# Loading part of wq on chosen DMA engines: 1152 columns in six loads against 1664 columns in five

## The chip, the cores and the metric

The kernel runs on one core of a Trainium2 chip. The core has five engines that run beside each other: TensorE (PE, with its weight loads shown apart as PEld), VectorE (DVE), ScalarE (ACT), GpSimd (POOL) and SyncE (SP), which here issues nearly all DMA loads. Sixteen DMA engines move the data. The metric is the device time in microseconds (us); lower is better.

## The reference

A decode step for eight sequences of one token each: attention over a cached window, then an MLP, each after a layer norm, each added to its input.

```python
def _A_ref(x, k_cache, v_cache, wq, wo):      # x [8,1,512], 32 query heads, 8 kv heads, Dh 128
    W = min(4096, max(256, Sk // 4))          # Sk = 8192, so the last 2048 positions
    q = (x @ wq)                              # wq [512, 4096]
    k = k_cache[:, :, Sk - W:, :]             # caches [8, 8, 8192, 128], repeated over 4 heads
    v = v_cache[:, :, Sk - W:, :]
    p = _softmax(einsum(q, k) * Dh ** -0.5)
    return einsum(p, v) @ wo                  # wo [4096, 512]

def _B_ref(x, w1, w2, w3, w4):                # the token shift of w1 and w2 is all zero for one token
    x1 = x + hs                               # hs is zero here
    return x1 + _gelu(_layernorm(x1) @ w3) @ w4    # w3 [512,1792], w4 [1792,512]

h = x + _A_ref(_layernorm(x), ...)
return h + _B_ref(_layernorm(h), ...)
```

Everything is bfloat16. Of the caches 64 MB are read, of the weights some 11 MB.

## The kernel before

The work is a stream of loads with the arithmetic behind it. SP issues the loads in an order written out by hand as a string of letters: K and V stand for one 2 MB piece of a cache each (four kv heads of one sequence, 2048 positions), Q for wq and O for the three pieces of wo; w3 and the three pieces of w4 come at the end. The order begins K, Q, K, K, V, K, V. Three buffers for K (knat) and three for V (vnat) are reused in turn, so that a load waits until the transposes (K, line 383) or the second product (V, line 504) of the piece three before are done.

K arrives with positions on the partitions. PE turns it (L383) into PSUM, ACT (L393) and DVE (L395) move it to kT_sb, PE multiplies it with the queries (L408), and after the softmax it multiplies the turned probabilities with V (L504). The result of each sequence is gathered in oW. At the end come wo (L553, L574), the layer norm, w3 (L678), the gelu (L704), w4 (L731), and the store (L788).

The queries need wq first. wq has 512 rows; row 4p+k is put on partition p as one of four stretches of 4096 columns of the tile wbig. The load of wbig leaves out the last QF = 1152 columns of the last stretch, that is, the last 1152 columns of every fourth row of wq (128 such pieces, one for each partition). These 128 pieces are loaded apart, by several small loads, into wqF, a view of the tile of w3, which is still free then.

The table FILL says how. Each entry (k, h, n) is one load of 4k pieces: k is the outer count of the source's access pattern, the pieces go to the partitions 32h to 32h+4k-1, and n is one of NF slots of wqF along the free dimension. With k = 8 a load runs on eight DMA engines, with k = 3 on three. All the other loads have 128 partitions and run on all sixteen. The function fills() walks the table; load_wq issues the loads (the helper at L207 issues every load); q_rows uses the same table three times: it copies the matching columns of the normalised x into xlnP (L282), turns them with PE (L287) into the same partitions and slots of xlnF (L292), and multiplies slot by slot with wqF (L313), after the products with wbig (L302), into the same PSUM banks. Partitions of a slot that hold no piece have to be zero in both: POOL clears xlnF (L216) and slots 1 and 2 of wqF (L217) at the start. A load into slot 0 doesn't wait for that, since slot 0 is filled in full; the others do.

The memsets on POOL stand ahead of the iota (L219), from which DVE makes the two identity matrices (L227, L228) and turn_f (L239), which the transposes of K need. q_rows stands on PE behind the transposes of the first four K tiles.

Of the kernel before, what the change touches and what calls it, by code (L numbers as in the profile page):

```python
# [6 lines left out]
dt = mybir.dt  # L7
# [4 lines left out]
B = 8  # L12
D = 512
H = 32
DH = 128
# [9 lines left out]
KC = D // 128  # L25
# [15 lines left out]
QW = H - 2 * NQ * R + 1  # L41
QE = QW + NQ * R + NQ * R + QW
AHEAD = NS
QF = 1152
FILL = ((8, 0, 0), (8, 1, 0), (8, 0, 1), (3, 1, 1), (3, 0, 2), (2, 1, 2))
NF = 3
KF = 64


class Engine:  # L50
# [29 lines left out]
def bass_sequential_preLN__sliding_block_cached__mixer_s_mlp__decode_kernel(  # L80
# [23 lines left out]
    with es:  # L104
        sb = lambda shape, dtype, name: es.enter_context(nc.sbuf_tensor(name, shape, dtype))
# [34 lines left out]
        rstd = sb([B, 1], dt.float32, "rstd")  # L140

        xlnF = sb([KF, NF, 32], dt.bfloat16, "xlnF")
        xlnP = sb([B, 4 * sum(k for k, _, _ in FILL)], dt.bfloat16, "xlnP")
        wqF = w3_sb[0:KF, 2:4, :].rearrange("p a n -> p (a n)")[:, 0:NF * QF].rearrange("p (s n) -> p s n", s=NF)
        xlnT = sb([128, KC, 32], dt.bfloat16, "xlnT")
        qrow = sb([128, 2, 512], dt.bfloat16, "qrow")
# [52 lines left out]
        sem_wf = S("sem_wf")  # L199
# [3 lines left out]
        PE, AC, DV, PO, SP = (Engine(S(n)) for n in ("s_pe", "s_act", "s_dve", "s_pool", "s_sp"))  # L203

        def dma(eng, dst, src, sem, *waits):
            def f(e):
                e.dma_start(dst, src).then_inc(sem, 16)  # L207
            eng.op(f, *waits, inc=False)
# [5 lines left out]
        PO.op(lambda e: e.memset(eps2[:], EPS * EPS))  # L214
        e_scr = PO.op(lambda e: e.memset(scratch[:], 1.0))
        e_fz = PO.op(lambda e: e.memset(xlnF[:], 0.0))  # L216
        e_wz = PO.op(lambda e: e.memset(wqF[:, 1:NF, :], 0.0))  # L217
        e_xz = PO.op(lambda e: e.memset(xlnT[:], 0.0))
        e_iota = PO.op(lambda e: e.iota(iota_f[:], [[1, 128]], base=0, channel_multiplier=-1,  # L219
                                        allow_small_or_imprecise_dtypes=True))  # L220
# [8 lines left out]
        e = DV.op(lambda e: e.bn_stats(st6[:, :], x_sb[:, :]), X)  # L229
        e = DV.op(lambda e: e.bn_aggr(mv[:, :], st6[:, :]), e)  # L230
        e = PO.op(lambda e: e.tensor_scalar(rstd[:, :], mv[:, 1:2], EPS, None, ALU.add), e)
        e = PO.op(lambda e: e.tensor_tensor(rstd[:, :], rstd[:, :], half[0:B, 0:1], ALU.pow), e)
# [8 lines left out]
        e = DV.op(lambda e: e.tensor_reduce(hsq[:, :], ident_f[:, :].rearrange("p (u h) -> p h u", u=4), AX.X, ALU.add))  # L241
# [7 lines left out]
        e = DV.op(lambda e: e.tensor_reduce(rows16[:, :].rearrange("p (t r) -> p t r", t=KQ),  # L249
                                            rows_f[:, :].rearrange("p (t s r) -> p t r s", t=KQ, s=NS), AX.X, ALU.add))  # L250
        a = rows16[:, :]
# [11 lines left out]
        e = PE.op(pe_xT, e_xln, e_idb)  # L263
# [5 lines left out]
        qT_ps = (o_rows, sm)  # L269
        fT_ps = pT_ps[:, 128:128 + NF * B]  # L270

        def fills():
            at = 0
            for k, h, n in FILL:
                yield k, slice(32 * h, 32 * h + 4 * k), n, at, slice(at, at + 4 * k)
                at += 4 * k

        def q_rows():
            for k, rows, n, at, where in fills():
                a = xln_b[:, :]  # L280
                cols = bass.AP(tensor=a.tensor, offset=a.offset + KC * at + KC - 1, ap=[a.ap[0], [KC, k], [KC * k, 4]])
                e_xP = DV.op(lambda e, cols=cols, where=where: e.tensor_copy(  # L282
                    xlnP[:, where].rearrange("b (e a) -> b e a", a=4), cols))

            def pe_fT(e):
                for k, rows, n, at, where in fills():
                    ins = e.matmul(fT_ps[rows, n * B:(n + 1) * B], xlnP[:, where], ident_b[0:B, 0:B],  # L287
                                   is_transpose=True, tile_position=(0, rows.start))
                return ins
            e = PE.op(pe_fT, e_xP)  # L290
            for k, rows, n, at, where in fills():
                e_fT = DV.op(lambda e, rows=rows, n=n: e.tensor_copy(xlnF[rows, n, 0:B], fT_ps[rows, n * B:(n + 1) * B]),  # L292
                             e, e_fz)
            out = []
            for j in range(2):
                def pe_q(e, j=j):
                    for kc in range(KC):
                        for u in range(4):
                            n = (4 * j + u) * R * DH
                            size = R * DH if kc < KC - 1 else max(0, min(R * DH, H * DH - QF - n))  # L300
                            if size:
                                ins = e.matmul(S_ps[j][32 * u:32 * (u + 1), 0:size], xlnT[:, kc, :], wq_v[:, kc, n:n + size],  # L302
                                               start=(kc == 0), stop=(kc == KC - 1 and size == R * DH),
                                               tile_position=(0, 32 * u), skip_group_check=True)
                    return ins

                def pe_qF(e):
                    for n in range(NF):
                        for u in range(4):
                            w = (u - 4) * R * DH + QF  # L310
                            lo = max(0, -w)
                            if lo < R * DH:
                                ins = e.matmul(S_ps[1][32 * u:32 * (u + 1), lo:R * DH], xlnF[:, n, :],  # L313
                                               wqF[:, n, w + lo:w + R * DH], start=False, stop=(n == NF - 1),
                                               tile_position=(0, 32 * u), skip_group_check=True)
                    return ins
                e_q = PE.op(pe_q, e_xT, (sem_wq, 16))
                if j == 1:
                    e_q = PE.op(pe_qF, e_fT, (sem_wf, 16 * len(FILL)))
                got = S_ps[j][:, :].rearrange("p (r d) -> p r d", r=R)  # L320
                for c in range(2):
                    if j == 0:
                        e = AC.op(lambda e, c=c, got=got: e.activation(qrow2[:, 0, :, c, :], got, ACT.Copy, scale=inv_sqrt_dh),
                                  e_q)
                    else:
                        e = DV.op(lambda e, c=c, got=got: e.tensor_scalar(qrow2[:, 1, :, c, :], got, inv_sqrt_dh, None,
                                                                          ALU.mult), e_q)
                out.append(e)
            return out, e_q
# [149 lines left out]
        a = ident_f[:, :].bitcast(dt.bfloat16)  # L479
# [126 lines left out]
        for p in range(AHEAD):  # L606
            pe_T(p)
            evict(p)
        e_qrow, e_q = q_rows()
        e_qT, e_qturn = q_turn()  # L610
        fill(0)
# [33 lines left out]
        def bc(a):  # L645
            return bass.AP(tensor=a.tensor, offset=a.offset, ap=[a.ap[0], [0, KC], [1, B]])


        e = DV.op(lambda e: e.tensor_reduce(hsum[:, :], vr(hT_ps[:, 0:NH]), AX.X, ALU.add), e_wo[-1])
# [41 lines left out]
        e = AC.op(lambda e: e.activation(s2[:, :], vsum[:, :], ACT.Sqrt, bias=eps2[:, :], scale=1.0), e_vs)  # L691
        e_r2 = DV.op(lambda e: e.reciprocal(r2[:, :], s2[:, :]), e)

        def bcf(t):
            a = t[:, :]
            return bass.AP(tensor=a.tensor, offset=a.offset, ap=[a.ap[0], [0, FH], [1, B]])
# [3 lines left out]
        for n in range(2):  # L700
            cs = slice(n * FH * B, (n + 1) * FH * B)
            e = DV.op(lambda e, n=n, cs=cs: e.tensor_tensor(v3(g_x[:, cs]), v3(y_ps[n][:, 0:FH * B]), bcf(r2),
                                                            ALU.mult), e_y[n], e_r2)
# [3 lines left out]
        e = PO.op(lambda e: e.tensor_scalar(r1[:, :], vsum[:, :], EPS * (1.0 + EPS), None, ALU.add), e_vs)  # L707
        e = PO.op(lambda e: e.tensor_tensor(r1[:, :], r1[:, :], half[:, :], ALU.pow), e)
        e = DV.op(lambda e: e.tensor_tensor(v3(xb[:, :]), v3(hc[:, :]), bc(r1[:, :]), ALU.mult), e)
# [49 lines left out]
        def load_wq():  # L759
            size = KC * H * DH - QF  # L760
            dma(SP, wbig[:, 0:size], A_wq.rearrange("(p k) n -> p (k n)", k=KC)[:, 0:size], sem_wq)
            for k, rows, n, at, where in fills():
                dma(SP, wqF[rows, n, :],
                    bass.AP(tensor=A_wq.tensor, offset=A_wq.offset + (KC * at + KC - 1) * H * DH + H * DH - QF,
                            ap=[[KC * H * DH, k], [KC * k * H * DH, 4], [1, QF]]), sem_wf, e_wz if n else None)

        def load_w3():
            dma(SP, w3_sb[:, :, :], B_w3.rearrange("(k p) f -> p k f", p=128), sem_w3, e_qturn)
# [8 lines left out]
        for kind in "KQKK" + 9 * "VK" + "VKKVKVKVVVOVOO":  # L777
            if kind == "Q":
                load_wq()
                continue  # L780
            {"K": load_k, "V": load_v, "O": load_wo}[kind](turn[kind])
            turn[kind] += 1
# [42 lines left out]
```

## Time and profile before

| | us |
|---|---|
| median of 3 runs | 193.34 (193.27 to 194.32) |
| the profiled execution: time | 193.18 |
| its span, first to last instruction | 191.9 |
| landing of the big load of wq (issued 1.42) | 17.53 |
| first product with the queries (L408) | 24.99 |
| landing of w3 | 185.03 |
| landing of the last piece of w4 | 189.32 |
| issue of the store | 190.50 |

| engine | busy us | share of the span |
|---|---|---|
| PE | 151.5 | 79% |
| DVE | 102.5 | 53% |
| ACT | 95.7 | 50% |
| POOL | 30.3 | 16% |

How to read it: the page of a profile divides the span into 40 slices and prints one digit a slice, tenths of busy time; 9 is 90% or more. The row DMA is the mean busy share of the 16 DMA engines. In the chain of work that ended last a row gives start, duration and what ran; a DMA's row runs from its issue to its landing. A row of the timeline gives start, duration, engine, line and operation, the tile written and the tiles read, and in brackets the idle time before it with what ended it. The trace also has a record of each DMA packet, with its queue, start, duration and size, and the times at which each load's semaphore counts up, once for every DMA engine that took part; neither names the engine.

### The profile page before, as it was taken

What the parts mean: (1) busy time and instruction counts of PE and PEld (TensorE: products, weight loads), DVE (VectorE), ACT (ScalarE), POOL (GpSimd) and SP (SyncE); (2) the same over time, 40 slices, a digit from 0 to 9 for tenths busy, and PEclk for the clock granted to TensorE, in tenths of its full rate; (3) what the DMA queues carried; (4) which work ended last, traced back from release to release, by engine and by line L of the source; (5) the groups of instructions that cost most, each with busy time, mean ns of one, the idle gap of its engine ahead of it and who ended that gap; (6) DMA issues with size and microseconds to landing.
All of it is one profiled execution on the core that took longest, in us unless ns stands there. A gap on an engine that the chain in (4) does not pass through costs nothing.

```text
span 191.9 us, 3209 instructions
## 1 busy us (share of the span) xinstructions
PE 151.5 (79%) x1325; PEld 94.9 (49%) x1325; DVE 102.5 (53%) x245; ACT 95.7 (50%) x124; POOL 30.3 (16%) x65
## 2 busy tenths in 40 slices
PE   0293879988878998699978896989898994777874
PEld 0281247664546555465655463746554661323453
DVE  2754314773386438543775275646853885535323
ACT  3081127776272927284559263754782767420331
POOL 8300020100230023002300230024002200140030
PEclk9999769999996999889999997999999999999985
DMA  6999999999999999999999999999999999999991
GB/s 220 422 406 432 437 420 427 434 437 424 434 429 427 430 430 427 429 430 430 437 430 420 437 430 429 420 437 424 437 434 425 434 434 432 408 430 428 411 409 75
DMA packets 6478, 79.38 MB, mean 414 GB/s; under 512 B 688, under 2 KB 704, under 8 KB 1856
## 3 DMA queue, kind: packets, MB, share of 16 engines
q1 hardware_dynamic: 6448, 79.18, 97.2%
q8 instruction: 10, 0.16, 0.3%
q14 instruction: 4, 0.03, 0.0%
q10 hardware_dynamic: 16, 0.01, 0.0%
HBM read 79.18 MB, written 0.01 MB: 413 GB/s over the span
## 4 chain that ended last, share of the span: by engine, by line
DMA 65%; PE 22%; DVE 6%; ACT 4%; SPq 1%; issue 1%; POOL 0%
DMA knat<-in_A_k_cache_dram 31%; DMA w_sb<-in_B_w_dram 16%; DMA vnat<-in_A_v_cache_dram 10%; PE kT_ps L383 9%; DMA wbig<-in_A_wq_dram 8%; PE S_ps L504 3%; ACT pT_sb L472 2%; PE S_ps L408 2%; PE o_rows L504 2%; DVE kT_sb L395 2%; ACT kT_sb L393 1%; PE S_ps L302 1%; PE sm L529 1%; PE kT_ps L678 1%; SPq L207 1%
## 5 line engine op out<-in xcount | busy, mean ns | idle before, releaser
L393 ACT ACTIVATE kT_sb<-kT_ps 128x1024 bf16<-128x1024 bf16 x64 | 65.6, 1025 | 65.3 <-PE kT_ps L383 65.2
L383 PE MATMUL kT_ps<-turn_f,knat 128*128 128x128 f32 x512 | 76.5, 293 | 12.2 <-DMA knat<-in_A_k_cache_dram 9.6
L383 PEld LDWEIGHTS kT_ps<-turn_f,knat 128*128 128x128 f32 x512 | 60.4, 149 | 31.9 <-issue 13.4
L395 DVE COPY kT_sb<-kT_ps 128x1024 bf16<-128x1024 bf16 x64 | 43.9, 686 | 34.7 <-PE kT_ps L383 34.6
L516 POOL TENSOR_TENSOR omask<-omask 128x256 f32<-128x256 f32 x14 | 10.2, 726 | 113.3 <-DVE omask L514 113.3
L408 PE MATMUL S_ps<-kT_sb,qblk 128*32 128x512 bf16 x256 | 26.5, 408 | 1.7 <-POOL qblk L350 1.1
L504 PE MATMUL o_rows<-vnat,pT_sb 128*64 128x512 bf16 x128 | 15.4, 381 | 5.4 <-ACT pT_sb L472 5.4
L472 ACT ACTIVATE pT_sb<-o_rows,own_f 128x512 bf16<-128x512 f32 x28 | 17.7, 694 | 1.8 <-PE o_rows L467 1.6
L504 PE MATMUL S_ps<-vnat,pT_sb 128*64 128x512 bf16 x112 | 13.4, 382 | 0.7 <-DMA vnat<-in_A_v_cache_dram 0.7
L504 PEld LDWEIGHTS o_rows<-vnat,pT_sb 128*64 128x64 bf16 x128 | 8.0, 109 | 11.5 <-issue 7.7
L408 PEld LDWEIGHTS S_ps<-kT_sb,qblk 128*32 128x32 bf16 x256 | 6.6, 93 | 13.4 <-issue 8.3
L514 DVE TENSOR_TENSOR omask<-o_rows,own_s 128x512 f32<-128x512 f32 x7 | 4.8, 686 | 12.5 <-PE o_rows L504 12.5
L514 DVE TENSOR_TENSOR omask<-S_ps,own_s 128x512 f32<-128x512 f32 x7 | 4.8, 692 | 11.7 <-PE S_ps L504 11.7
L350 POOL COPY qblk<-qT 64x64 bf16<-64x64 bf16 x16 | 5.0, 312 | 27.0 <-DVE qT L342 16.4
L504 PEld LDWEIGHTS S_ps<-vnat,pT_sb 128*64 128x64 bf16 x112 | 5.8, 110 | 6.8 <-issue 1.6
L529 PE MATMUL sm<-oacc,sel_o 128*128 128x256 f32 x16 | 7.2, 537 | 0.6 <-DVE oX L536 0.6
L440 ACT ACTIVATE E_sb<-S_ps,negM 128x512 f32<-128x512 f32 x8 | 5.5, 689 | 2.4 <-DVE negM L436 2.4
L259 PE MATMUL sm<-ident_b,xln_b 8*128 8x8 bf16 x4 | 0.3, 176 | 8.0 <-DVE xln_b L234 8.0
L517 POOL TENSOR_TENSOR oacc<-omask 128x128 f32<-128x128 f32 x14 | 6.4, 455 | 1.1
L559 ACT ACTIVATE orow<-kT_ps 128x512 bf16<-128x512 f32 x1 | 0.6, 597 | 11.2 <-PE kT_ps L553 11.2
L431 DVE TENSOR_REDUCE mblk<-S_ps 128x1 f32<-128x512 f32 x8 | 5.5, 682 | 0.8 <-PE S_ps L408 0.8
L453 DVE STREAM_TRANSPOSE PT_sb<-P_sb 128x512 bf16<-128x512 bf16 x8 | 5.6, 702 | 0.0
(120 smaller groups left out, 102.6 us busy)
## 6 DMA issues: line engine op xcount, KB each, us to landing
knat<-in_A_k_cache_dram SPq DMA_DIRECT2D x16, 2048.0 KB, 19.3
vnat<-in_A_v_cache_dram SPq DMA_DIRECT2D x15, 2048.0 KB, 20.3
wbig<-in_A_wq_dram SPq DMA_DIRECT2D x1, 3808.0 KB, 16.1
wbig<-in_A_wo_dram SPq DMA_DIRECT2D x2, 1024.0 KB, 22.9
knat<-in_A_v_cache_dram SPq DMA_DIRECT2D x1, 2048.0 KB, 20.4
wbig<-in_A_wo_dram SPq DMA_DIRECT2D x1, 2048.0 KB, 24.7
w_sb<-in_B_w_dram SPq DMA_DIRECT2D x1, 1792.0 KB, 30.7
w_sb<-in_B_w_dram SPq DMA_DIRECT2D x1, 1024.0 KB, 32.6
```

Of the source, the lines that this page charges most:

```text
L383: ins = e.matmul(kT_ps[i % 2][:, n * 256:(n + 1) * 256].bitcast(dt.float32), knat[:, j % NK, c * DH:(c + 2) * DH].bitcast(dt.float32), tur ...
L393: e_lo[i] = AC.op(lambda e: e.activation(kT_sb[:, i % NKT, 0:W // 2], kT_ps[i % 2][:, 0:W // 2], ACT.Copy), e_Tlo[i], e_QK.get(i - NKT))
L395: e_hi[i] = DV.op(lambda e: e.tensor_copy(kT_sb[:, i % NKT, W // 2:W], kT_ps[i % 2][:, W // 2:W]), e_Thi[i], e_QK.get(i - NKT))
L408: ins = e.matmul(S_ps[b % 2][32 * t:32 * (t + 1), :], qblk[:, b % 2, KQ * q + t, half, at:at + H], kT[:, :, t, :, half], start=(q == 0 and ...
L431: e = DV.op(lambda e: e.tensor_reduce(mblk[:, 0:1], S_ps[b % 2][:, :], AX.X, ALU.max), e_QK[G * b + G - 1], e_mz)
L453: e_PT[b] = DV.op(lambda e: e.transpose(PT_sb[:, :], P_sb[:, :]), e_P[b], e_wide.get(b - 1))
L472: e_pT[b, t] = AC.op(lambda e: e.activation(pT_sb[:, b % 2, :, H * t:H * (t + 1)], bank[:, :].rearrange("p (n y) -> p n y", n=NN), ACT.Cop ...
L504: ins = e.matmul(bank[64 * u:64 * (u + 1), :], pT_sb[:, b % 2, n, :].rearrange("p (x q) -> p q x", q=NQ)[:, q, :], v_tile(m)[:, n * 512:(n ...
L514: free[at] = DV.op(lambda e: e.tensor_tensor(omask[:, :, :], bank.rearrange("p (s d) -> p s d", s=NS), own, ALU.mult), e_PV[m], e_acc.get( ...
L516: e = PO.op(lambda e: e.tensor_tensor(omask[:, 0:2, :], omask[:, 0:2, :], omask[:, 2:4, :], ALU.add), free[at], pool[-1])
L517: pool[-1] = e_acc[m] = PO.op(lambda e: e.tensor_tensor(acc, omask[:, 0, :], omask[:, 1, :], ALU.add), e, e_O.get(b - 2))
L529: e_O[b] = PE.op(lambda e: e.matmul(O_ps, sel_o[:, :], oacc[:, b % 2, :, :].rearrange("p q d -> p (q d)"), start=True, stop=True), e_acc[N ...
```

## The change

QF grows from 1152 to 1664 columns, so the big load has 512 columns fewer. FILL's entries get a fourth number m, the pieces for each step of the outer count, which was always 4. The table has five loads instead of six: two of twelve times four pieces (partitions 0 to 47 and 64 to 111 of slot 0), two of three times four (partitions 0 to 11 and 32 to 43 of slot 1), and one of eight single pieces (partitions 64 to 71 of slot 1). There are two slots instead of three, and they reach over 128 partitions instead of 64. As slot 0 is no longer full, all of wqF is cleared, and every load apart waits for that.

```diff
-QF = 1152
-FILL = ((8, 0, 0), (8, 1, 0), (8, 0, 1), (3, 1, 1), (3, 0, 2), (2, 1, 2))
-NF = 3
-KF = 64
+QF = 1664
+FILL = ((12, 4, 0, 0), (12, 4, 2, 0), (3, 4, 0, 1), (3, 4, 1, 1), (8, 1, 2, 1))
+NF = 2
+KF = 128
...
-        e_wz = PO.op(lambda e: e.memset(wqF[:, 1:NF, :], 0.0))
+        e_wz = PO.op(lambda e: e.memset(wqF[:, :, :], 0.0))
...
-            for k, h, n in FILL:
-                yield k, slice(32 * h, 32 * h + 4 * k), n, at, slice(at, at + 4 * k)
-                at += 4 * k
+            for k, m, h, n in FILL:
+                yield k, m, slice(32 * h, 32 * h + m * k), n, at, slice(at, at + m * k)
+                at += m * k
...
-                            ap=[[KC * H * DH, k], [KC * k * H * DH, 4], [1, QF]]), sem_wf, e_wz if n else None)
+                            ap=[[KC * H * DH, k], [KC * k * H * DH, m], [1, QF]]), sem_wf, e_wz)
```

The uses of fills() in q_rows take m in place of the 4 in the same way.

## The prediction

> **What bounds the kernel now.** I read the page's forty slices first, then its DMA parts, the chain that ended last and the timeline at both ends, and last the single DMA packet records and landing counts of the trace.
>
> ```profile
> DMA  6999999999999999999999999999999999999991
> ...
> DMA packets 6478, 79.38 MB, mean 414 GB/s; under 512 B 688, under 2 KB 704, under 8 KB 1856
> ...
> q8 instruction: 10, 0.16, 0.3%
> q14 instruction: 4, 0.03, 0.0%
> ```
>
> The DMA engines have no free slice between the first and the last: bytes set the pace. The two instruction queues look negligible here and are not, as the packet records show below. The chain's end, and the timeline there:
>
> ```profile
> 154.37 30.67 DMA w_sb<-in_B_w_dram
> 185.03 0.05 issue
> 185.08 1.99 PE kT_ps L678 x56
> ...
> 188.99 0.80 PE S_ps L731 x20
> ```
>
> ```profile
> 189.36 0.14 PEld L731 LDWEIGHTS S_ps<-w_sb,qrow 128*32 128x32 bf16 x8 [0.21 <-DMA w_sb<-in_B_w_dram]
> 189.82 0.56 ACT L741 ACTIVATE orow<-S_ps 8x128 bf16<-8x128 f32 x2 [2.23 <-PE S_ps L731]
> 189.82 0.60 DVE L743 CAST orow<-S_ps 8x128 bf16<-8x128 f32 x2 [1.74 <-PE S_ps L731]
> 190.50 0.32 SPq L788 DMA_DIRECT2D out_dram<-orow  x1
> ```
>
> The W3 load releases L678 at 185.03, and the last piece of W4 (landed 189.32) releases the last eight matmuls at 189.36. Both are landings in one ring order, so the end follows the engine that lands last.
>
> The packet records tell which one that is. A load is cut over its engines; each engine runs its packets back to back, each starting 3 or 4 ns before the one ahead ends (16,384 B take 611 ns on every engine, in nearly all of 4,234 packets). So the records fall into 16 chains, and the number of 2,304-byte rows sorts them. End of each chain's last packet in us (the landing follows 0.29 later):
>
> ```
> 24 rows, two engines (0, 1)      188.29  188.88
> 20 rows, one engine (2)          188.30
> 12 rows, five engines (3 to 7)   187.13  187.30  188.49  188.80  188.84
> no row, eight engines (8 to 15)  186.09  186.47  187.51  187.54  187.63  187.68  187.69  189.03
> ```
>
> The numbers 0 to 15 are my labels by how many loads a chain takes part in. Within a class the ends differ by instruction fetches: a 16 KB packet of q8 sets its chain back 1.41 us (186.09 against 187.51), an 8 KB one of q14 0.55 to 0.85. Ten q8 packets go round eight chains: two of class 3 to 7, then six of class 8 to 15. The first, at 26.66, hits the fifth of those six, and the ninth, at 180.90, hits it again. That chain, with no row at all, is the one at 189.03, which ends the kernel; the tenth fetch comes at 187.62, too late to matter.
>
> **The change part by part.** The time of the profiled execution is 193.18, of which 191.9 is span; the median of the runs shown is 193.34, 0.16 above, and I carry differences over to that.
>
> The big load of wq loses 512 columns a row: 30,464 B at 1,128 ns against 16,384 at 611 is 0.0367 ns a byte, so 1,024 B less save 38 ns, and eight rows an engine save 0.30 us on all sixteen.
>
> The rows apart have 3,328 B. No packet of that size exists; on the line through 4,096 B (159 ns) and 3,584 B (140 ns) it takes 131 ns, less the 3.5 of overlap 127; the old row takes 93, so 89.5. Engines 0 to 2 get 4+4+4+4+1 = 17 rows, 3 to 7 get 9, 8 to 11 get 8, 12 to 15 none. New against old:
>
> - 0, 1: 17×127 = 2.16 for 24×89.5 = 2.15, with the 0.30: -0.28
> - 2: 2.16 for 1.79: +0.08
> - 3 to 7: 1.14 for 1.07: -0.23
> - 8 to 11: 1.02 for nothing: +0.72
> - 12 to 15: -0.30
>
> That holds if a row costs the same whoever else is writing. In the old loads apart engine e writes partitions 4e to 4e+3 or the same 32 above, and no other engine does either. The new twelve-engine loads are different. In the first, engines 8 to 11 write partitions 32 to 47, beside engines 0 to 3 at 0 to 15. In the second, all twelve write 64 to 111, the half that engines 8 to 15 fill in every full load, four of which are then on K rows already. In the last, eight engines write eight neighbouring partitions. Before shows no such row. Bounds: from below nothing (eight engines write x into eight neighbouring partitions at 44 ns a packet, unstretched); from above the output store, where eight engines read eight such partitions and the 1,024-byte packets take 45 to 101 ns, a factor of 2.3. I take a factor of 2, two writers that halve one place: x is one short packet an engine, which may hide a queue, while here each engine puts four rows of 3,328 B on end. It costs:
>
> - 0, 1, 2: eight rows doubled, 1.02, and their last single row, one of four at one place, some 0.25: +0.99, +0.99, +1.35
> - 3: as much, +1.04; 4 to 7: four rows doubled against the K rows of 12 to 15, 0.51, and 0.25: +0.53
> - 8 to 11: eight rows, 1.02: +1.74, on two of them up to 0.5 more
> - 12 to 15: 0.51 lost while shared: +0.21
>
> The new ends: 188.88+0.99 = 189.87; 188.30+1.35 = 189.65; 188.84+0.53 to 1.04 = 189.4 to 189.9; 187.69+1.74 to 2.24 = 189.4 to 189.9; 189.03+0.21 = 189.24. Several land together near 189.9 and the latest of so many lies a little above: 190.08 against 189.03, +1.05. The tail behind the last landing is unchanged work and moves with it.
>
> The Trainium skill, "SBUF — State Buffer", section "Door 1: The DMA port swizzle", states that partitions 32 apart share one of 16 DMA ports of about 27 GB/s and that 64 partitions get no more bandwidth than 32. By that rule the sharing above is real and the sum is about the +1.05; the trace of before neither shows nor denies it, for its rows apart kept to their own places.
>
> What goes away on compute: one matmul of 512 columns at L302, one of 128 at L313, one transpose, two small DVE copies. All lie in the stretch that waits for wq; none bears on the end, for the loads never wait for them. The other parts that the change touches stand at the start:
>
> ```profile
> 0.94 2.02 POOL L217 MEMSET w_sb<- 64x2304 bf16 x1
> ...
> 2.03 4.55 SPq L207 DMA_DIRECT2D w_sb<-in_A_wq_dram  x6
> ...
> 3.15 0.24 POOL L219 IOTA iota_f<- 128x128 f32 x1
> ...
> 6.63 1.23 SPq L207 DMA_DIRECT2D knat<-in_A_k_cache_dram  x2
> ...
> 8.59 5.60 PE L383 MATMUL kT_ps<-turn_f,knat 128*128 128x128 f32 x32 [0.26 <-DVE turn_f L239]
> ...
> 14.21 0.54 SPq L207 DMA_DIRECT2D knat<-in_A_k_cache_dram  x1
> ...
> 17.57 2.85 PE L302 MATMUL S_ps<-wbig,xlnT 128*32 128x512 bf16 x30 [1.86 <-DMA wbig<-in_A_wq_dram]
> ```
>
> The memset grows from 2,304 to 3,328 elements a partition: 2.02×1.44 = 2.92, ending 3.86. Now every load apart waits for it, and behind that wait on SP stand K1, K2, V0. Five issues at 0.72 end near 7.5 instead of 6.58, so K1 is issued 0.9 late; engines run on K0 and the big load until about 16.7, a cover of 9 us. On POOL the iota, the identities made from it on DVE, turn_f and the first transposes (L383) all slip 0.9; K3's issue, behind them, goes from 14.21 to 15.1, while V0 occupies the rings until 33.97. L287 moves to 16.4, ahead of wq's landing at 17.2. Each cost is zero; without the covers the largest would be 0.9. If the rows apart land 1 us later than L302 needs, QK starts up to 0.7 late, and K4's issue (32.24) with it; V1 occupies the rings until 43.68, so again nothing.
>
> **The rivals.** *Rows do not share* (not slower): the writes go in at the engines' own rate, as x's packets do. Then the last chains are 188.73 (the one with two fetches, if it is among 12 to 15) and 188.60: -0.30, 193.04, inside the bound. It decides if the new rows show 131 ns throughout.
>
> *The fetches fall elsewhere.* I put the twice-hit chain among 12 to 15 because the round goes upward: after two of 3 to 7 it is the fifth of six, hence at least 12. If the changed program's round begins elsewhere, or goes downward, the double hit falls on one of 8 to 11: 189.03+0.72, 194.06, without sharing; 189.03+1.74 to 2.24, 195.1 to 195.6, with it. The spread of the runs, 194.32 beside 193.27, is about what a double hit on class 3 to 7 would make (187.1+2.82 = 189.9), so the round may well move from one execution to another.
>
> *No double hit that counts, and no sharing*: the last would be engine 0 or 1 without fetch, 188.29-0.28 = 188.01, -1.02 on 189.03: 192.3.
>
> That the load isn't spread as said speaks from no row: the old loads fall into exactly the classes their outer counts name.
>
> **How the numbers follow.** A measurement of this kernel can tell about 0.5%, 0.97 us. Sharing with the round as it is: 0.45, time 193.34+1.05 = 194.4, own range 193.8 (half as dear) to 194.7 (factor 2.3); 0.27 of it above the bound, 0.18 below. No sharing: 0.21, same. Round moved without sharing: 0.07, same; with sharing 0.20, slower. No hit that counts: 0.07, faster. Sums: slower 0.47, same 0.46, faster 0.07. The range 193.0 to 195.3 leaves out the last case and half of the dear one.
>
> **What would show it.** In the changed profile: 3,328-byte packets of engines 0 to 3 and 8 to 11 at 131 or near 260 ns; K1's landings spread by about 3.5 us instead of 2.25 (21.98 to 24.23); which class ends last; the last landing near 190.4. A last landing at or below 189.3 proves the sharing wrong. A PE wait for knat that is much longer than now before 60 us would show that a cover failed.

## The result and the profile after

The changed kernel takes 193.79 us (median of 22 runs, 193.59 to 194.05), the kernel before 193.32 (22 runs): 0.47 us more, a ratio of 1.0021 with a 95% interval of 1.0015 to 1.0027. The profiled executions differ by 0.61 (193.79 against 193.18). The forecast was +1.05. A ratio, here and below, is worked out from the fast runs of both kernels and is not the ratio of the two medians; the only slow runs are two of second_at_64, 197.62 and 201.02 us.

The page of the changed kernel, the rows of the DMA engines and of the instruction queues:

```profile
DMA  6999999999999999999999999999999999999992
...
DMA packets 6484, 79.38 MB, mean 412 GB/s; under 512 B 694, under 2 KB 710, under 8 KB 1862
...
q8 instruction: 10, 0.16, 0.3%
q14 instruction: 4, 0.03, 0.0%
```

Still no free slice, the same bytes, 14 instruction fetches as before. Its chain that ended last, and the end of its timeline:

```profile
154.66 31.02 DMA w_sb<-in_B_w_dram
185.72 1.99 PE kT_ps L678 x56
188.37 1.05 PE S_ps L731 x32
189.63 0.79 PE S_ps L731 x24
```

```profile
189.99 0.14 PEld L731 LDWEIGHTS S_ps<-w_sb,qrow 128*32 128x32 bf16 x8 [0.20 <-DMA w_sb<-in_B_w_dram]
190.45 0.56 ACT L741 ACTIVATE orow<-S_ps 8x128 bf16<-8x128 f32 x2 [2.22 <-PE S_ps L731]
190.45 0.59 DVE L743 CAST orow<-S_ps 8x128 bf16<-8x128 f32 x2 [1.74 <-PE S_ps L731]
191.14 0.31 SPq L788 DMA_DIRECT2D out_dram<-orow  x1
```

The chain is the same as before, each step 0.63 to 0.69 later: the last eight matmuls start at 189.99 instead of 189.36, the last landing is at 189.95 instead of 189.32. So the whole difference is in when the DMA engines land their last bytes. Where it arises is seen in the windows around the rows apart and K1 (the last three numbers of a row are the granted clock of TensorE, the mean busy share of the DMA engines, and GB/s counted by packets that start in the window). Before, then after:

```profile
16.50:22.00 5.50, 4.43 (x41) 1.57 (x42) 0.43 (x3) 1.08 (x2) 0.00 (x0) 0.69 0.99 417
22.00:26.00 4.00, 2.06 (x17) 0.88 (x16) 1.64 (x4) 0.00 (x0) 1.25 (x4) 0.90 1.02 438
26.00:189.00 163.00, 138.20 (x1215) 86.91 (x1218) 90.45 (x208) 88.53 (x114) 22.87 (x43) 0.95 1.00 425
```

```profile
16.50:22.00 5.50, 3.27 (x46) 1.50 (x46) 2.36 (x13) 1.09 (x2) 0.00 (x0) 1.00 1.05 387
22.00:26.00 4.00, 2.54 (x19) 1.81 (x20) 0.76 (x3) 0.24 (x1) 1.24 (x4) 0.86 0.98 418
26.00:189.00 163.00, 136.45 (x1187) 84.72 (x1188) 90.53 (x208) 88.04 (x114) 22.94 (x43) 0.95 1.00 427
```

From 26 us on the two are alike. Between 16.5 and 22 the engines are as busy as before (1.05 against 0.99), yet move 387 GB/s instead of 417: packets take longer. The single packets say how. Of the 128 rows of 3,328 B, 71 take 131 ns, the rest up to 336. And K1, eight packets of 16,384 B on each engine, takes 4.87 us on every chain of before (8 times 607, and the semaphore packet). A chain is, as in the prediction, the packets of one engine in a row. In the changed kernel K1 takes:

```
chains by first packet of K1     K1, us         end of last packet, us (before: by class)
four at 16.60 to 16.72 (12-15)   5.64           186.76 188.06 188.19 189.67   (0 rows: 186.09 to 189.03)
nine at 17.68 to 18.00 (3-11)    5.26 to 5.66   187.50 to 189.28              (0 and 12 rows)
three at 19.31 to 19.38 (0-2)    4.89 to 4.90   188.60 189.14 189.22          (20, 24 rows: 188.29 188.30 188.88)
```

All packets of rows and K1 together have 12.2 us of excess over 131 and 611 ns, a mean of 0.76 for each of the 16 chains; chain by chain it is some 0.6 to 1.0. The last chain is again one of 12 to 15 that is fetched on twice (at 27.81 and 181.41), 189.67. On it the big load ends 0.25 earlier than on the last chain of before, K1 takes 0.77 longer, and the first fetch sets it back by 1.52 instead of 1.41: together the 0.63 by which the end moved. Why that fetch costs more is not shown; it costs 1.52 to 1.58 in every kernel here that writes the rows elsewhere than before does, and 1.41 in before, start_only and before_pause.

### The profile page after: what moved, and what is told of

Its sections match the earlier page's. It is cut to its first block, busy times and chain, and to the rows that moved or that the text cites. A ratio compares the mean times of both kernels' runs of the same rounds, so it can differ in the third digit from the quotient of the medians.

```text
span 192.5 us, 3200 instructions
## 1 busy us (share of the span) xinstructions
PE 150.4 (78%) x1322; PEld 95.2 (49%) x1322; DVE 102.3 (53%) x243; ACT 95.5 (50%) x124; POOL 31.2 (16%) x65
## 4 chain that ended last, share of the span: by engine, by line
DMA 65%; PE 19%; DVE 5%; ACT 5%; POOL 2%; SPq 2%; issue 1%; POOLq 0%
DMA knat<-in_A_k_cache_dram 32%; DMA w_sb<-in_B_w_dram 16%; DMA vnat<-in_A_v_cache_dram 10%; PE kT_ps L383 8%; DMA w_sb<-in_A_wq_dram 7%; PE S_ps L504 3%; ACT pT_sb L472 2%; ACT kT_sb L393 2%; PE o_rows L504 2%; PE S_ps L408 2%; DVE kT_sb L395 2%; SPq L207 2%; POOL w_sb L217 1%; PE kT_ps L678 1%; PE S_ps L731 1%
## 5 line engine op out<-in xcount | busy, mean ns | idle before, releaser
L383 PEld LDWEIGHTS kT_ps<-turn_f,knat 128*128 128x128 f32 x512 | 61.1, 150 | 33.1 <-DMA knat<-in_A_k_cache_dram 15.3
L504 PE MATMUL o_rows<-vnat,pT_sb 128*64 128x512 bf16 x128 | 15.9, 390 | 5.9 <-ACT pT_sb L472 5.9
L529 PE MATMUL sm<-oacc,sel_o 128*128 128x256 f32 x16 | 6.6, 502 | 0.6 <-DVE oX L536 0.6
```

The costliest lines, as they stand in the source:

```text
L383: ins = e.matmul(kT_ps[i % 2][:, n * 256:(n + 1) * 256].bitcast(dt.float32), knat[:, j % NK, c * DH:(c + 2) * DH].bitcast(dt.float32), tur ...
L504: ins = e.matmul(bank[64 * u:64 * (u + 1), :], pT_sb[:, b % 2, n, :].rearrange("p (x q) -> p q x", q=NQ)[:, q, :], v_tile(m)[:, n * 512:(n ...
L529: e_O[b] = PE.op(lambda e: e.matmul(O_ps, sel_o[:, :], oacc[:, b % 2, :, :].rearrange("p q d -> p (q d)"), start=True, stop=True), e_acc[N ...
```

## The experiments

All times are beside runs of before on the same chip, with the ratio to them. Experiments on the loads write FILL as (k, m, first partition, slot); the code around it is that of the changed kernel, with its longer memset and its waits, and q_rows turns a load that starts at partition 32 and reaches over 64 in two pieces. The diffs show the lines that matter, cut at "...", with the old FILL in the same form.

**start_only: the start without the loads.**

```diff
+QF = 1152
+FILL = ((8, 4, 0, 0), (8, 4, 32, 0), (8, 4, 0, 1), (3, 4, 32, 1), (3, 4, 0, 2), (2, 4, 32, 2))
+NF = 3
```

> The loads of before (2,304-byte rows, the same destinations), but wqF cleared over all 128 partitions and every load apart waiting for that, as in the changed kernel. If the later start has its cover, as the prediction has it: 193.3, within 0.1 of before, rows at 93 ns, the last landing at 189.3. If the start itself costs what the changed kernel lost: 193.8.

Measured 193.56 against 193.41, ratio 1.0003 (0.9982 to 1.0024); its profiled execution took 193.31, with 113 of 128 rows at 93 ns, K1 at 4.87 us (4.89 on one chain) and the last landing at 189.36, against 189.32 in before. The start is covered, as forecast.

```profile
16.50:22.00 5.50, 3.57 (x50) 1.68 (x51) 3.10 (x16) 1.21 (x3) 0.00 (x0) 1.00 1.01 420
```

On this chip both kernels had a second level about 0.9 above the first, before in 14 of 35 runs; so the medians say little, and the packets more. The lower level of before, its other 21 runs, has its median at 193.29.

**second_at_64: one of the old loads to the other half.**

```diff
-FILL = ((8, 4, 0, 0), (8, 4, 32, 0), ...
+FILL = ((8, 4, 0, 0), (8, 4, 64, 0), ...
```

> As start_only, and of the first two eight-engine loads the second goes to partitions 64 to 95 instead of 32 to 63; the reads are the same to the byte. Places shared on the write side: engines 0 to 7 then write into the half that the eight engines without rows are filling with K1; four rows of 84 KB in all, about 0.34 us lost on each of the engines 8 to 15 and as much on 0 to 7, some rows well over 93 ns, the last landing 0.3 later, 193.6. Reads by twelve engines at once as the cause of the stretch in the changed kernel: nothing changes, 193.3 and 93 ns.

Measured 194.45, ratio 1.0029 (1.0008 to 1.0051). The reads are those of before to the byte, and still only 61 of 128 rows take 93 ns, against 113 in start_only; others reach 392. So the stretch comes from where the rows are written, not from twelve engines that read. But the loss isn't where it was expected: K1 is long on all 16 chains, 5.4 to 5.5 us. In the profiled execution something more was seen:

```profile
16.50:22.00 5.50, 3.54 (x49) 1.58 (x49) 2.08 (x10) 1.09 (x2) 0.00 (x0) 1.00 1.02 372
22.00:26.00 4.00, 1.82 (x17) 1.09 (x18) 0.77 (x3) 0.00 (x0) 1.25 (x4) 1.00 1.02 393
...
28.00:60.00 32.00, 25.65 (x209) 16.98 (x206) 17.64 (x38) 18.39 (x23) 3.62 (x8) 0.95 1.01 431
```

Long after the last of the rows (19.5), up to 26, the rate stays at 393 and the engines are at 1.02: every packet of every chain takes 675 to 684 ns instead of 611. At 26.51 the first instruction fetch takes one chain out for 1.1 us, and from 26.9 on all the others are at 611 again. So K1's length here is mostly this step (six packets of 70 ns more, some 0.4 of 0.6 us on the chains without rows), and not the meeting of the writes itself. The four runs that lie in the lower level, 193.47 to 193.67, stand some 0.3 above the lower level of before, near the 193.6 that was expected.

**twelve_at_32: the changed loads, other partitions.**

```diff
-FILL = ((12, 4, 0, 0), (12, 4, 64, 0), (3, 4, 0, 1), (3, 4, 32, 1), (8, 1, 64, 1))
+FILL = ((12, 4, 32, 0), (12, 4, 32, 1), (3, 4, 0, 0), (3, 4, 0, 1), (8, 1, 96, 0))
```

> The changed kernel with both twelve-engine loads at partitions 32 to 79 (of slots 0 and 1), the three-engine loads at 0 to 11, the last one at 96 to 103; the reads are those of the changed kernel. If engine e has its own place at 4e to 4e+3 and 32 above (counting 64 to 127 on from there), nobody shares in the two large loads: rows at 131 ns but for the last single ones, engines 12 to 15 no longer held up, and the sum without sharing holds: 0.30 less than before, 193.0. Reads by twelve engines as the cause: rows as stretched as in the changed kernel, 193.8.

```profile
16.50:22.00 5.50, 3.37 (x44) 1.64 (x45) 2.50 (x10) 1.09 (x2) 0.00 (x0) 1.00 1.06 440
```

The profiled execution took 193.01; 440 GB/s in the window; 116 of 128 rows at 131 ns; K1 4.90 us on chains 12 to 15 and on seven of the nine chains 3 to 11 (5.13 and 5.18 on the other two, each with one packet of about 860 ns); last chain 188.87, against 188.73 by the unshared sum. Rows and K1 have 1.5 us of excess in all, against 12.2 in the changed kernel. So the sum without sharing holds once the partitions are right. The times on this chip were in two levels: three runs at 193.0 to 193.1, nine at 193.9 to 194.7, hence a median of 194.02 and a ratio of 1.0011 (0.9988 to 1.0034). What the upper level is, no profile of this kernel caught.

**late_ninth: no second fetch on the last chain.** Of each group of 16 second products of the first seven sequences 12 are left out, so this kernel does not compute the whole result.

```diff
-                for n in range(NN):
+                for n in (range(NN) if b == LAST else (0, 1, NN - 2, NN - 1)):
```

> The changed kernel, leaving out 12 of the 16 second products (L504) of each group in the first seven sequences: 168 matmuls and as many weight loads fewer on PE, so that the ninth 16 KB instruction fetch falls behind the last landing. If the chain that is fetched on twice sets the end: it lands 1.4 earlier, the end passes to the next chain, 0.4 earlier (189.28 against 189.67 in the packet records), 193.4. If the double fetch is no cause: 193.8.

Measured 193.59 (193.27 to 193.87), ratio 0.9996 (0.9979 to 1.0013). That ratio can't be set beside the 1.0021 of the changed kernel, for on this chip 14 of 35 runs of before are in the upper level and none of these 12; beside the lower level of before it is 0.30 more, where the changed kernel had 0.47 and 0.38 more on two other chips. In the packet records no chain has two 16 KB fetches before the end (the eighth comes at 183.77, the ninth at 189.30), and the last chain is now one of 0 to 2, at 189.56. So the twice-fetched chain did set the end of the changed kernel, at 189.67, and the end passed on when its second fetch went. But only 0.11 of the expected 0.4 was gained in this profile, where K1 took 5.70 us instead of 5.64 on the chains without rows; by time alone the difference is too small to show more.

**after_again, and a short pause.** The changed kernel beside before on a third chip, and three kernels with one small load issued on ACT's queue at 18.2 to 19.4 us, two rows of 8 KB on two engines, to see whether it ends the step of 681 ns.

```diff
+                        if c:
+                            dma(AC, w4_sb[0:2, 0:8, :].rearrange("p k n -> p (k n)"),
+                                A_wo.rearrange("(p j) n -> p (j n)", j=8)[0:2, :], sem_b)
```

> The changed kernel as it is, on the chip of this set, beside before. Shared places plus the double fetch: its profile again with about half of the 3,328-byte rows over 131 ns, chains 12 to 15 some 0.6 later than before, 193.7 to 193.9. If the higher level near 194.2 that before showed in 14 of 35 runs of the last set is a property of the chip and not of the kernel, the changed kernel shows it here as well, near 194.6.

> Before, with one small load added on ACT's queue behind L323, at about 19.4: two rows of 8 KB on two engines, into a part of w4's tile that is loaded much later. The profile of second_at_64 had all sixteen chains at 681 ns a packet from about 17.5 until the first instruction fetch at 26.5 took one chain out, then 611 at once. Theory: packets of all engines can fall into a step in which each takes 681, and any short interruption of one engine ends it; this, lasting until the first fetch, is the upper level near 194.2. Then this kernel shows the lower level alone, 193.3 to 193.5, its own cost being 0.3 on two chains that do not end the kernel. Rival, the upper level comes from elsewhere: it stays in about 4 runs of 10.

> second_at_64 with the same small load at 19.4. If a short interruption ends the step of 681 ns: packets at 611 from about 20 on in the profile, and no run above 194.0 (8 of 12 were without it), 193.6. If not: 681 until the first fetch, 194.4.

> twelve_at_32 with the same small load. If its upper runs near 194.1 (9 of 12) were the step of 681 ns: all runs near 193.0 to 193.2, below before by 0.2 to 0.3. If they were something else: two levels as without it.

The diff shows the load alone; the loads of w4 wait for it. On this chip before had one level only (31 runs, 193.17 to 193.61), so the pause had little to end and its theory wasn't tested. after_again: 193.72, ratio 1.0016 (1.0008 to 1.0025), 71 of 128 rows at 131 ns, K1 of chains 12 to 15 at 5.50 us, last chain 189.52: the same picture on another chip, and no second level. before_pause: 193.45, 1.0008 (0.9999 to 1.0017). second_at_64_pause: 193.80, 1.0029 (1.0017 to 1.0040); its packets were back near 615 by 19 us, before the small load ran at 21.9, and three of eight runs were above 194.0 all the same, where none was expected. Without the step its profile shows what the meeting alone does: 85 of 128 rows at 93 ns, the longest 418, and K1 at 5.1 us on most chains without rows, some 0.2 more than in before. twelve_at_32_pause: 193.21, 0.9991 (0.9983 to 1.0000), all 11 runs below 193.4. Whether the pause or the chip removed the upper level is open.

**two_at_64, first_twelve_at_0, three_at_96: who pays.** The question left was the spread: do the engines pay whose places are written by two, or all?

```diff
 two_at_64:          (..., (2, 4, 64, 2))  instead of (..., (2, 4, 32, 2)), the rest as start_only
 first_twelve_at_0:  ((12, 4, 0, 0), (12, 4, 32, 1), (3, 4, 0, 1), (3, 4, 64, 0), (8, 1, 96, 0))
 three_at_96:        ((12, 4, 32, 0), (12, 4, 32, 1), (3, 4, 0, 0), (3, 4, 96, 1), (8, 1, 96, 0))
```

> As start_only, but of the old loads only the last one (two engines, four rows each) goes to partitions 64 to 71 instead of 32 to 39. Loss by place: engines 0 and 1 now write where two of the chains without rows are writing K1; four rows of 93 ns each, 0.34 lost on these four chains and nothing on the other twelve, whose K1 packets stay at 611; 193.3. Loss shared by all: packets of other chains are stretched as well in that stretch of time (about 18.5 to 19.5), each of the 16 losing about 0.1; 193.4.

> As twelve_at_32, but the first twelve-engine load is back at partitions 0 to 47 of slot 0, where engines 8 to 11 write beside engines 0 to 3, and the second three-engine load goes to 64 to 75, beside chains 8 to 10. Nobody writes where 12 to 15 write. Loss by place: K1 of those four chains runs at 611 throughout, the chain that is fetched on twice ends as in twelve_at_32 (188.9), the end may pass to 8 to 11 (188.4 + 0.5 to 1.0); 193.0 to 193.4. Loss shared by all: the first K1 packets of chains 12 to 15 stretched too, about 0.4 lost on them, the twice-fetched chain at 189.2 to 189.3, 193.3 to 193.5.

> first_twelve_at_0 moved two loads against twelve_at_32: the first twelve-engine load to 0 to 47, and the second three-engine load to 64 to 75. This one moves the three-engine load alone (to 96 to 107), with both twelve-engine loads at 32 to 79. If partitions 32 to 47 beside 0 to 15 were what cost first_twelve_at_0 about 1 us on all chains: K1 of chains 12 to 15 takes 4.9 to 5.1 us, the last landing is near 189.2, 193.0 to 193.2. If the three-engine load into the other half was: K1 of those chains takes near 5.9, the last landing is near 190.2, 194.1.

The windows of first_twelve_at_0, then of three_at_96:

```profile
16.50:22.00 5.50, 3.36 (x47) 1.51 (x47) 1.53 (x7) 1.09 (x2) 0.00 (x0) 1.00 1.06 366
```

```profile
16.50:22.00 5.50, 3.19 (x48) 1.43 (x48) 2.70 (x15) 1.09 (x3) 0.00 (x0) 1.00 1.05 394
```

first_twelve_at_0 is the slowest of all, 194.17, ratio 1.0038 (1.0025 to 1.0052), though nobody writes where 12 to 15 write, by the places that the expectation gives to the engines. K1 of these four chains takes 5.92 us, 1.05 more than alone; of 3 to 11, 5.63 to 5.91; the rate is 366 GB/s, and from 21 us on packets take 611 ns again, so it isn't the step of second_at_64. Loss by place alone is refuted: all pay, some 0.9 to 1.2 us each with the rows, and more than the 0.4 that I gave the other theory. three_at_96 moves only one of the two loads (to 96, not 64) and lies between the two ends of its expectation: K1 of 12 to 15 takes 5.41 to 5.44, last landing 189.62, 193.61, ratio 1.0010 (1.0001 to 1.0020). So three engines that write four rows each into the other half cost all 16 about 0.5 us. By difference the remaining 0.5 of first_twelve_at_0 goes with partitions 32 to 47 beside 0 to 15; no run moved that load alone. two_at_64 is the mildest: 193.41, 1.0001 (0.9992 to 1.0010). Between 19.0 and 19.5 K1 packets take 725 and 727 ns on two chains without rows and 627 to 635 on nearly all others, 0.12 us a chain on the two and some 0.02 on the rest: two chains pay more, as loss by place would have it (and one of the two engines that write there has 0.21 more in its rows), and all the others a little, too little to time. Why eight smaller rows cost so much less than the twelve of three_at_96 is not shown.

**twelve_at_32_wide: a better version.**

```diff
-QF = 1664
+QF = 1792
```

> twelve_at_32 with QF = 1792 instead of 1664. Each engine loads 256 B less a row of the big load, 0.08 us; the twice-fetched chain, without rows, ends 0.08 earlier, near 188.8; engines 0 to 2 have 17 rows of 3,584 B instead of 3,328, +0.16 - 0.08, near 188.65. 192.95 where no step of 681 ns comes in, that is 0.3 to 0.4 below before; a second level near 194.0 if it does.

Measured 193.05 (11 runs, 192.88 to 193.20) against 193.39 for before on the same chip, ratio 0.9982 (0.9974 to 0.9991): 0.34 below before. The changed kernel, on another chip, had 193.79.

```profile
16.50:22.00 5.50, 3.28 (x49) 1.50 (x50) 2.67 (x13) 1.09 (x2) 0.00 (x0) 1.00 1.05 436
```

436 GB/s in the window, near twelve_at_32, and no second level on this chip, where before had none either (21 runs). The split of the pieces over engines that the change brought is a gain once its loads go where twelve_at_32 puts them, the two large ones to partitions 32 to 79, where each engine keeps to its own place by the expectation's map. How it does on the chip with two levels wasn't run; there twelve_at_32 was in the upper one in 9 of 12 runs.

## Why the prediction was right or wrong

The forecast was wrong in size and in path. The direction held, but +1.05 was forecast, over 0.5%, and +0.47 measured, 0.2%; and the chain that ends the kernel is not one of those that were to end it.

- *The bound, and which chain ends the kernel*: the bound was right, the end moved with the last landing (0.63 each). The chain was not: one of 0 to 11 was to be the last, near 189.9, and the one that is fetched on twice at 189.24. It is the last again, at 189.67 and 189.52 in the two profiles of the changed kernel; late_ninth took its second fetch away and the end passed on.
- *Big load, -0.30*: right; 1,091 ns for 1,128 in most packets, first landing 16.65 for 16.99.
- *Row price, 131 ns unshared*: right, to the nanosecond, in 71 rows here and 116 in twelve_at_32.
- *The start at zero*: right, by start_only. Of the changed kernel's timeline:

```profile
0.91 2.87 POOL L217 MEMSET w_sb<- 128x3328 bf16 x1
...
3.81 3.84 SPq L207 DMA_DIRECT2D w_sb<-in_A_wq_dram  x5
...
7.71 1.23 SPq L207 DMA_DIRECT2D knat<-in_A_k_cache_dram  x2
...
9.42 6.47 PE L383 MATMUL kT_ps<-turn_f,knat 128*128 128x128 f32 x32 [0.27 <-DVE turn_f L239]
...
15.91 0.54 SPq L207 DMA_DIRECT2D knat<-in_A_k_cache_dram  x1
...
17.33 1.85 PE L302 MATMUL S_ps<-wbig,xlnT 128*32 128x512 bf16 x29
...
24.11 0.62 PE L408 MATMUL S_ps<-kT_sb,qblk 128*32 128x512 bf16 x8 [1.13 <-POOL qblk L350]
```

  The memset and the first transposes are about where the sum put them, and K1's issue slipped 1.08 instead of 0.9. K3's issue slipped 1.70 instead of 0.9, as the transposes themselves took 6.47 instead of 5.60; V0 still covers it. The first product with the queries, which I had up to 0.7 late, came at 24.11, 0.88 early: L302 took 1.85 us instead of 2.85, with 29 matmuls recorded instead of 30 and at a granted clock of 1.00 instead of 0.69 in the window from 16.5.
- *Sharing is real*: right, and shown: twelve_at_32 against the changed kernel (131 ns again, last chain 188.87 for 189.67), second_at_64 against start_only with the same reads.
- *What sharing costs, and whom*: the step that failed. I doubled the rows of the engines that meet at one place and charged them alone: 1.0 to 1.5 on 0 to 3 and 8 to 11, 0.8 on 4 to 7, 0.5 on 12 to 15. Summed over all chains that is 15.2 us; measured 12.2, so the total was not far off. But all 16 pay, each some 0.6 to 1.0. K1's landings, which were to spread over 3.5 us instead of 2.25, spread over 2.04 (22.65 to 24.69). The chains of 0 to 2, which were among those to end the kernel, ended 0.31, 0.34 and 0.85 later than before and not 0.99, 0.99 and 1.35; those of 8 to 11, which were to end at 189.4 to 189.9, ended by 189.28. The twice-fetched chain, which was to be 0.21 later, was 0.63 later and stayed last: its loss by sharing was 0.77 and not 0.51, the big load gave it 0.25, and its first fetch took 0.10 more, a term that the sum did not have. So the kernel came out slower by another path than the one forecast, and the right direction owes something to luck.

By the Trainium skill, "SBUF — State Buffer", section "Door 1: The DMA port swizzle", partitions 32 apart share a port and those 64 apart don't, and on the places the runs agree with it: twelve_at_32, in which nearly nobody shares by its map, moves 440 GB/s, and three_at_96, which sends one small load into the other half, 394. With rows 32 apart written by two engines as well, first_twelve_at_0 moves 366. But the engines with a place to themselves paid too, 1.05 us on four of them in first_twelve_at_0; that is what the sum had left out.

- *The rivals*: that rows don't share fell. That the round of fetches begins elsewhere fell too for these profiles: first and ninth fetch were on one of 12 to 15 again. The level of 194.32 in one early run, which I read as such a shift, may be the second level seen later; that wasn't caught in a profile of before.

What stays open: through what the slow-down spreads to all engines, and what the second level is, which on one chip took 14 of 35 runs of before, on three others none of 65, and one of the 22 beside the changed kernel. The step of 681 ns until the first fetch, seen once, has about the right size for it (some 10% of 8 us), no more.

## What to carry to other kernels

Where all DMA engines are busy from end to end, the time is that of the one that ends last: add up each engine's bytes and its instruction fetches from the packet records, not only the mean. When a load runs on fewer engines than 16, look where each engine writes as well as how many bytes it carries; let every engine keep to the partitions that it writes in full loads, for here all engines paid, not only those that met. A layout that balances bytes by the sum can lose through its destinations what it gains; here other partitions for the same loads, with 128 columns more, turned 0.47 us of loss into 0.34 of gain on a chip with one level.

## What the runs showed of the hardware that was not expected

- A few rows that engines write to the places of others slow all 16 engines: in first_twelve_at_0 K1 took 5.92 us instead of 4.87 on four engines whose places, by the map of the expectation, nobody else wrote.
- After such a meeting all engines can stay at 675 to 684 ns a 16 KB packet for some 7 us, until the first instruction fetch on one engine; that the fetch ended it is not shown (second_at_64, one execution).
